# Sixteen short steps of dummy transposes in TensorE's list, and three other banks, in a decay-attention and mixture kernel

## The chip, the cores and the metric

The kernel runs on one core of one Trainium2 chip. The metric is device time in microseconds (us) of one execution, the median over several runs. Five engines work side by side, each through its own list of instructions in order: TensorE (PE in the profile, with its weight loads as PEld), VectorE (DVE), ScalarE (ACT), GpSimd (POOL) and SyncE (SP), which issues most of the DMAs. They wait for one another through semaphores.

## The reference, cut to what matters

```python
# r, k, v: (4, 8, 768, 48); w, u: (8, 48)
for t in range(S):
    kt, vt, rt = (k[:, :, t], v[:, :, t], r[:, :, t])
    cur = np.einsum('bhd,bhe->bhde', u[None] * kt, vt)
    y[:, :, t] = np.einsum('bhd,bhde->bhe', rt, state + cur)
    state = w[None, :, :, None] * state + np.einsum('bhd,bhe->bhde', kt, vt)
x = y.transpose(0, 2, 1, 3).reshape(B, S, H * D)     # (4, 768, 384)
logits = x @ w_gate                                   # 4 experts, the 2 largest are kept
for e in range(E):
    q, k, v = x @ wq[e], x @ wk[e], x @ wv[e]         # 384 -> 64
    a = softmax(scale * q @ k.T, causal)              # 768 x 768
    out += gate[e] * (a @ v @ wo[e])
```

Everything is float32. The first part is a linear attention with a decay by channel; its output is the input of a mixture of four small softmax attentions with causal mask.

## The kernel before, in words

The sequence of each of the four batches is cut into six chunks of 128 rows, so there are 24 chunks, n = 0 to 23. The first part works chunk by chunk; its steps have names that begin with `a_`. The second part works on groups of three chunks, G = 0 to 7, with steps that begin with `m_`.

For chunk n the first part does this. `load_chunk`, `load_vh` and `load_vs` bring k, r and v. `a_decay` (L470) multiplies k and r with powers of w, `a_ku` (L479, POOL) forms the products for the row's own term. `a_transpose` (L497) turns k and r on TensorE, 16 short transposes on line L513 (for chunk 0 on L506 and L524), and copies them to SBUF on ScalarE as kt (L519), rt (L532) and rx (L536). `a_quarters` (L541) forms the scores inside the chunk (32 matmuls on L552) and the state sums (up to 32 on L560). `a_mask` (L565) masks the scores on VectorE (sm, L569), `a_own` (L488) forms the own term on VectorE (L492, L494), `a_sum` (L599) adds the state on VectorE (z, L608) and multiplies it for the next chunk on POOL (L612). `a_out` (L573) forms the output with 64 small matmuls on L585 and L589, `a_add` (L591) adds the own term on VectorE (L596). `a_xt` (L614) turns the result, six transposes on L620 into the two banks of a `psb` home; ScalarE copies it to xt_hi (L623); and `a_xl` (L626) subtracts on VectorE, reading the same two banks again, which gives xt_lo (L631).

The second part starts with `m_values` (L678; nine matmuls on L686 for each chunk), `m_proj` (L651; nine on L661), `m_gate`, `m_scores` (L738), `m_weigh`, `m_turn` (L770), `m_av` (L791) and `m_out`. `hi_v`, `lo_v` (L451, L453), `hi_qk` and `lo_qk` (L438) split the weights into two parts, on ScalarE and VectorE, in the same early stretch.

The order is written out by hand. `ORDER` (L16) is a list of words, each the name of a step with its arguments; a step that yields has several words. The loop at L839 goes through the words, and every instruction of a step is appended to the list of its engine at that moment. Behind a slash stand hexadecimal digits: the homes that the step takes, in turn, by `take` (L245). TensorE's outputs live in eight PSUM banks of 512 columns. A `ps` home is one bank. A `psb` home i is the two banks i and i+1, because both are cut from one tile:

```python
SHARED = {"ps": 512, "psb": 512}
        if name in SHARED:
            return whole[:, i * SHARED[name]:i * SHARED[name] + WIDTH[name]]
```

So `a_xt,0/0` writes columns of banks 0 and 1, and `a_quarters,2/45` writes bank 4 for its first parity and bank 5 for its second, with the parities alternating from the first matmul on. A step that writes a bank which an earlier word reads waits until that reading is done.

`keep` (L357) is a step with no result that anyone reads: it takes a bank and turns the identity matrix into it, four transposes of 128x128. The kernel before has one such step at the very start, `keep,2`, on L360, ahead of the warm-up matmuls (L319).

Of the kernel before, what the change touches and what calls it, by code (L numbers as in the profile page):

```python
# [27 lines left out]
load_qk,0/5 a_quarters,3/26 m_values,0,0/1 a_xt,2/4 a_xt,2 a_xl,2 a_decay,4,1 a_transpose,4/0 m_values,0,1/7 hi_qk,0  # L28
lo_qk,0 load_chunk,5 a_decay,5,0 a_own,3/1 load_chunk,5 a_decay,5,1 load_vs,3 a_ku,5/0 a_ku,5 m_values,0,2/4 load_vs,3
a_transpose,4/0 m_proj,0,1,0/5 a_transpose,4/02 a_mask,3/03 m_proj,0,1,0/1 m_values,0,1 a_sum,3 a_sum,3/0 m_values,0,2  # L30
make_after m_gate,0/001 m_values,0,1/1 load_vh,5 m_proj,0,0,1/1 m_proj,0,0,1/2 load_vh,4 load_chunk,6 m_proj,0,1,0
m_proj,0,0,0/7 a_own,5/00 m_values,0,2 m_proj,0,0,0/0 a_decay,6,0 m_proj,0,0,0 load_chunk,6 m_values,0,0 a_out,3 a_add,3
a_transpose,5/4 load_chunk,7 load_chunk,7 load_vs,5 load_vs,5 m_proj,0,0,1 a_transpose,5/1 a_ku,4/0 a_transpose,5/11
m_scores,0,0,2/37 m_scores,0,0,2/41 m_scores,0,0,2/34 a_quarters,4/62 a_mask,4/03 m_scores,0,0,0/31 m_scores,0,0,0/15
a_xt,3/4 a_xt,3/1 m_scores,0,0,0/03 load_o,0/6 make_sums,0 m_scores,0,0,2 a_quarters,5/7 load_vs,4 m_gate,0
m_scores,0,0,1/31 a_ku,6/1 hi_o,0 a_xl,3/1 m_values,1,0/4 a_sum,4 a_sum,4/2 a_decay,6,1 a_mask,5/12 load_vs,4
m_scores,0,0,1/20 m_scores,0,0,0 m_scores,0,0,0 m_gate,0/501 a_ku,4 a_sum,5 load_vs,6 a_out,4 m_proj,0,1,1/3 load_vs,6
m_scores,0,0,2 load_chunk,8 m_scores,0,0,1/47 m_scores,0,0,1 m_weigh,0,0/3 a_out,5 a_own,4/1 load_vh,8 m_values,1,0/0
a_add,4 a_xt,4/1 m_proj,0,1,1 a_ku,6 m_proj,0,1,1 m_weigh,0,0 m_turn,0,0,0/5 m_values,1,0/2 m_scores,0,0,1 a_xt,4
m_scores,0,1,2/43 m_turn,0,0,0/0 a_add,5 m_scores,0,1,1/07 a_xl,4 m_weigh,0,1/2 a_xt,5/1 a_xt,5 m_weigh,0,1  # L40
a_transpose,6/5 a_decay,7,0 a_transpose,6/0 m_scores,0,1,1/01 a_xl,5 m_values,1,1/0 load_o,1/2 hi_o,1 lo_o,1
a_transpose,6/20 m_values,1,1 m_values,1,1 m_scores,0,1,2/50 m_proj,1,1,0/1 a_decay,7,1 m_scores,0,1,1/15 m_proj,1,0,0/4
m_scores,0,1,2/22 m_scores,0,1,2 load_vh,6 a_own,6/21 load_chunk,8 m_scores,0,1,2 a_decay,8,1 m_turn,0,1,0/5
m_scores,0,1,0/07 m_scores,0,1,0/33 m_scores,0,1,1 a_decay,8,0 a_ku,8/0 m_scores,0,1,0/44 m_proj,1,1,0 m_proj,1,0,0/0
a_ku,8 m_proj,1,1,0 m_proj,1,0,0 m_scores,0,1,0 a_quarters,6/3 m_values,1,2/0 m_scores,0,1,1 a_mask,6/30 a_sum,6/2
a_sum,6 m_proj,1,0,1/7 m_weigh,0,2/2 m_turn,0,1,0/2 load_vh,7 m_values,1,2 m_gate,1/100 m_values,1,2 m_scores,0,1,0
m_weigh,0,3/0 a_transpose,8/5 m_proj,1,0,1/1 m_proj,1,0,1 a_out,6 load_chunk,9 a_transpose,8/0 a_sum,6/1
a_transpose,8/01 m_weigh,0,2 m_turn,0,2,0/0 load_vs,7 lo_o,0 m_scores,1,0,0/47 m_turn,0,2,0/4 load_chunk,9 m_weigh,0,3
m_turn,0,3,0/5 m_turn,0,3,0/1 a_ku,7/1 a_add,6 m_scores,1,0,0/56 m_scores,1,0,0/24 m_scores,1,0,0 a_decay,9,0
m_scores,1,0,2/20 m_scores,1,0,2/02 a_transpose,7/4 m_scores,1,0,0 m_av,7,1,0,3 a_xt,6/6 a_xt,6/0 m_scores,1,0,2/30  # L50
a_xl,6/0 load_chunk,10 m_proj,1,1,1/2 m_gate,1 m_gate,1/110 a_ku,7 a_transpose,7/1 a_transpose,7/10 a_own,7/60
m_proj,1,1,1 m_proj,1,1,1 m_values,2,0/3 m_scores,1,0,2 m_scores,1,0,1/40 m_scores,1,0,1/07 m_scores,1,0,1/11
a_quarters,7/7 m_scores,1,0,2 a_sum,7 m_values,2,0/0 m_scores,1,0,1 m_av,0,0,0,3/2 m_scores,1,0,1 make_sums,1
a_mask,7/10 m_weigh,1,0/1 load_chunk,10 m_av,0,0,0,3/1 m_av,0,0,0,3/0 m_values,2,0/0 a_quarters,8/45 m_av,0,1,0,3/0
a_mask,8/23 a_sum,7/0 a_sum,8 m_av,0,1,0,3/0 load_vh,10 load_vh,9 m_av,0,1,0,3/1 load_vs,7 a_out,7 a_add,7 m_weigh,1,0
m_turn,1,0,1/2 load_vs,8 m_turn,1,0,1/3 load_vs,8 load_vs,9 m_weigh,1,1/1 a_decay,10,1 a_own,8/1 m_scores,1,1,2/06
a_xt,7/2 a_xt,7 m_scores,1,1,2/03 a_out,8 m_turn,1,0,0/0 a_xl,7 m_scores,1,1,0/23 m_turn,1,0,0/5 a_add,8 m_weigh,1,1
a_sum,8/2 m_turn,1,1,1/4 m_scores,1,1,2/15 a_xt,8/0 a_xt,8 m_turn,1,1,1/0 a_decay,10,0 load_vs,9 m_scores,1,1,0/36
a_xl,8 m_out,0,1/6 m_turn,1,0,2/4 m_out,0,1/0 load_vh,11 m_turn,1,1,0/0 m_turn,1,0,2/2 m_turn,1,1,0/1 load_chunk,12
a_transpose,10/6 m_scores,1,1,0/22 a_transpose,10/1 m_scores,1,1,1/24 a_transpose,10/22 load_chunk,11 a_decay,11,0  # L60
a_decay,9,1 m_scores,1,1,1/47 m_scores,1,1,1/54 m_scores,1,1,2 m_out,0,0/0 m_out,0,0/1 a_quarters,10/21 m_turn,1,1,2/6
a_mask,10/20 a_ku,9/1 a_transpose,9/3 m_turn,1,1,2/4 m_proj,2,0,0/5 a_ku,10/0 a_ku,10 a_own,10/1 load_chunk,11
load_chunk,14 m_proj,2,0,1/0 a_decay,11,1 a_decay,12,0 a_ku,11/0 load_chunk,14 a_ku,9 a_transpose,9/0 a_transpose,9/11
a_quarters,9/67 m_proj,2,1,1/4 m_scores,1,1,0 m_out,0,1 a_sum,9 a_decay,14,1 load_vh,12 a_sum,9/1 m_proj,2,1,0/3
m_scores,1,1,2 m_proj,2,0,0/2 m_proj,2,0,0 a_sum,10 a_mask,9/31 a_out,9 m_scores,1,1,1 m_weigh,1,2/3 m_weigh,1,2
m_scores,1,1,0 m_scores,1,1,1 m_proj,2,1,1/0 m_proj,2,0,1/0 m_proj,2,1,0 m_weigh,1,3/0 m_weigh,1,3 m_proj,2,1,0
# [810 lines left out]
```

## Time and profile before

| what | value |
|---|---|
| runs | 305.86 us median of 3 (305.4 to 306.49) |
| the profiled execution's own time | 306.47 us |
| its span (first to last instruction) | 304.7 us |
| busy PE / DVE / ACT / POOL | 292.3 / 206.0 / 213.6 / 173.2 us |
| mean granted TensorE clock | 0.976 of full speed |
| chain that ended last | PE 80%, DVE 6%, ACT 5%, issue 2%, POOL 1% |

The profile page has the busy time of each engine, the span in 40 slices of 7.6 us with the clock that was granted to TensorE in each, and the chain of work that ended last. The trace behind it can be asked for the instructions of an engine in order of time, for the busy time and clock of any stretch, and for who waited for whom. [...]

### The profile page before, as it was taken

The page shows a single profiled execution, that of the slowest core. Times are in us where ns is not written, and L with a number is a line of the kernel's source. Part 1 is how long each engine was busy: PE and PEld are TensorE (multiplying, and loading weights), DVE is VectorE, ACT ScalarE, POOL GpSimd, SP SyncE. Part 2 cuts the span into 40 slices and gives each one's busy share as a digit, 9 for nine tenths or more (in the row PEclk, how much of TensorE's full clock was granted, in tenths as well). Part 3 has the DMA queues.
Part 4 walks back from the last instruction along what each step waited for, and adds up shares of the span by engine and source line. Part 5 has one row for each costly group of instructions (what it writes and reads, how often), then busy time and mean ns, then how long its engine had stood idle before and what let it go on. Part 6 is the DMA issues. An engine that isn't in the chain of part 4 may idle for free.

```text
span 304.7 us, 13045 instructions
## 1 busy us (share of the span) xinstructions
PE 292.3 (96%) x5518; PEld 248.8 (82%) x5518; DVE 206.0 (68%) x676; ACT 213.6 (70%) x509; POOL 173.2 (57%) x227
## 2 busy tenths in 40 slices
...
PEclk9965999999999999999999999999999999999999
...
GB/s 157 219 188 118 80 55 107 120 122 25 108 56 166 72 41 159 105 17 105 93 106 1 80 69 141 111 123 102 41 3 41 54 2 31 0 25 56 23 60 77
DMA packets 103310, 24.83 MB, mean 81 GB/s; under 512 B 99794, under 2 KB 103252, under 8 KB 103252
## 3 DMA queue, kind: packets, MB, share of 16 engines
...
q8 instruction: 43, 0.70, 1.0%
...
## 4 chain that ended last, share of the span: by engine, by line
PE 80%; DVE 6%; ACT 5%; issue 2%; POOL 1%; ACTq 0%; DVEq 0%; POOLq 0%
PE banks L661 16%; PE banks L791 11%; PE banks L738 10%; PE banks L686 9%; PE banks L770 8%; PE banks L589 4%; PE banks L552 4%; PE banks L585 4%; PE banks L814 4%; PE banks L513 3%; PE banks L816 3%; PE banks L815 3%; PE banks L560 2%; PE banks L620 2%; ACT rx L536 1%
## 5 line engine op out<-in xcount | busy, mean ns | idle before, releaser
L761 POOL TENSOR_SCALAR pr<-pr,f,gate 128x128 f32<-128x128 f32 (+5 forms) x96 | 67.7, 719 | 72.2 <-DVE f L755 48.7
L743 DVE CUSTOM_DVE_ANT_0 pr<-banks,after 128x256 f32<-128x256 f32 (+5 forms) x96 | 56.5, 620 | 26.7 <-PE banks L738 18.8
L748 ACT ACTIVATE pr<-pr,nm 128x512 f32<-128x512 f32 (+5 forms) x96 | 63.4, 663 | 8.1 <-DVE nm L743 7.7
L773 ACT ACTIVATE pt<-banks 128x768 f32<-128x768 f32 (+1 forms) x64 | 45.6, 731 | 14.8 <-PE banks L770 14.1
L738 PE MATMUL banks<-tk,tq 64*128 64x384 f32 (+3 forms) x384 | 41.5, 338 | 0.2
L791 PE MATMUL banks<-pt,vv 128*64 128x384 f32 (+2 forms) x324 | 40.7, 393 | 0.7 <-DVE yl L800 0.7
L791 PEld LDWEIGHTS banks<-pt,vv 128*64 128x64 f32 x324 | 20.6, 136 | 16.6 <-issue 12.3
L661 PE MATMUL banks<-xt_hi,wqk_hi 128*128 128x384 f32 x96 | 33.5, 349 | 0.6 <-DVE nm L743 0.6
L738 PEld LDWEIGHTS banks<-tk,tq 64*128 64x128 f32 x384 | 30.7, 186 | 3.5 <-issue 1.4
L770 PE MATMUL banks<-ident,pr 64*128 64x64 f32 x672 | 31.6, 227 | 0.9 <-DVE xt_lo L631 0.5
L661 PE MATMUL banks<-xt_hi,wqk_lo 128*128 128x384 f32 x96 | 32.3, 337 | 0.0
L661 PE MATMUL banks<-xt_lo,wqk_hi 128*128 128x384 f32 x96 | 32.3, 336 | 0.0
L770 PEld LDWEIGHTS banks<-ident,pr 64*128 64x128 f32 x672 | 26.2, 139 | 7.1 <-issue 4.2
L612 POOL TENSOR_TENSOR z<-z,w 128x192 f32<-128x192 f32 x20 | 10.1, 506 | 30.4 <-DVE z L608 19.4
L483 POOL TENSOR_TENSOR ku<-kdbuf,uw 128x384 f32<-128x384 f32 x24 | 25.0, 1045 | 2.6 <-DVE banks L492 1.9
L476 POOL TENSOR_TENSOR rdbuf<-rdbuf,tab_r 128x384 f32<-128x384 f32 x22 | 22.7, 1038 | 5.7 <-DMA rdbuf<-in_r_dram 5.7
L585 PE MATMUL banks<-vhbuf,sm 64*64 64x48 f32 x384 | 25.7, 226 | 0.1
L485 POOL TENSOR_TENSOR ku<-ku,rdbuf 128x384 f32<-128x384 f32 x24 | 24.9, 1039 | 1.3
L585 PE MATMUL banks<-vsbuf,sm 64*64 64x48 f32 x384 | 25.2, 226 | 0.0
L686 PE MATMUL banks<-wv_hi,xt_hi 128*128 128x260 f32 x72 | 22.4, 312 | 0.1
L585 PEld LDWEIGHTS banks<-vhbuf,sm 64*64 64x64 f32 x384 | 21.5, 141 | 0.3 <-issue 0.3
L476 POOL TENSOR_TENSOR kdbuf<-kdbuf,tab_k 128x384 f32<-128x384 f32 x21 | 21.5, 1027 | 0.0
(125 smaller groups left out, 723.9 us busy)
## 6 DMA issues: line engine op xcount, KB each, us to landing
...
```

The costliest lines, as they stand in the source:

```text
L476: nc.gpsimd.tensor_tensor(t[:, :, :D], t[:, :, :D], (tab_k, tab_r)[which], op=OP.mult)
L483: nc.gpsimd.tensor_tensor(ku, kd[:, :, :D], uw, op=OP.mult)
L585: nc.tensor.matmul(o, st["sm", n][par][rows, p // 2, i], values, start=fresh, stop=True)
L661: nc.tensor.matmul(ps, a[:, t, m0:m0 + P], x[:, t, :], start=i == 0, stop=i == n - 1)
L686: nc.tensor.matmul(ps, x[:, t, cols], a[:, t, :], start=m == 0, stop=m == n - 1)
L738: nc.tensor.matmul(ps[par][:, n0:n1], tq[rows, part, q], tk[rows, key, n0:n1], start=i == 0, stop=i == 2)
L743: nc.vector.tensor_tensor_reduce(pr_[:, :N], ps[par], after[:, S - N:], 1.0, 3e38, op0=OP.add, op1=OP.min, accum_out=nm)
L748: nc.scalar.activation(pr_[:, :N], pr_[:, :N], AF.Exp, bias=nm, scale=-1.0, accum_out=sums[:, e, j, 0:1])
L761: nc.gpsimd.tensor_scalar(p[:, :N], p[:, :N], f[:, i], gate[:, i, e:e + 1], op0=OP.mult, op1=OP.mult)
L770: nc.tensor.transpose(both[:, x, half], mg[G]["p", e, j][rows, i * C:(i + 1) * C], ident[rows, rows])
L773: nc.scalar.activation(pt.rearrange("s (x half c) -> s x half c", x=n, half=2), both, AF.Copy)
L791: nc.tensor.matmul(psy[par * HD:par * HD + HD, j0 * C:j1 * C], vv[:, i % GC, e, :], mg[G]["t", e, i][:, (j0 - max(0, i - g * GC)) * C:(j1 ...
```

## The change

Sixteen steps `keep,50` to `keep,65` are put into `ORDER`, and `keep` makes two transposes for them in place of four, 32 transposes in all. Two steps stand between `a_quarters,1` and `a_xt,0`, five between `a_quarters,2` and `a_out,1`, six between `a_out,1` and `a_xt,1`, and three between `a_out,2` and `m_values,0,0`, seen from TensorE's list. No other word changes its place. Three words get other homes: `a_quarters,1` takes banks 7 and 0 in place of 2 and 7, `a_xt,0` takes `psb` home 5 (banks 5 and 6) in place of home 0 (banks 0 and 1), and `a_own,1` takes the second `ownv` buffer in place of the first. `a_quarters,2/45` keeps banks 4 and 5, and `a_xl,0` stands ahead of it in the list as before.

```diff
-load_vh,1 a_quarters,1/27 a_sum,0 a_sum,0/0 a_own,0/0 a_add,0 a_mask,1/12 a_ku,2/0 a_ku,2 a_transpose,2/0
-a_transpose,2/02 load_vh,2 a_xt,0/0 a_own,1/0 load_chunk,3 a_xt,0/0 load_vs,1 a_sum,1 a_sum,1/1 load_chunk,3 a_xl,0/0
-load_vs,1 a_quarters,2/45 a_mask,2/30 a_decay,3,1 a_sum,2 a_out,1 a_add,1 a_xt,1/0 load_v/6 hi_v load_vh,3 a_decay,3,0
-a_ku,3/1 a_ku,3 a_transpose,3/2 load_chunk,4 lo_v load_vs,2 load_vs,2 a_sum,2/2 a_out,2 a_own,2/1 a_add,2
-a_transpose,3/0 a_transpose,3/21 a_xt,1 m_values,0,0/3 load_qk,1/3 hi_qk,1 a_xl,1 lo_qk,1 load_chunk,4 a_decay,4,0
...
+load_vh,1 a_quarters,1/70 a_sum,0 a_sum,0/0 a_own,0/0 a_add,0 a_mask,1/12 a_ku,2/0 a_ku,2 a_transpose,2/0
+a_transpose,2/02 load_vh,2 keep,50/1 keep,51/2 a_xt,0/5 a_own,1/1 load_chunk,3 a_xt,0/0 load_vs,1 a_sum,1 a_sum,1/1
+load_chunk,3 a_xl,0/0 load_vs,1 a_quarters,2/45 a_mask,2/30 a_decay,3,1 a_sum,2 keep,52/1 keep,53/2 keep,54/3 keep,55/6
+keep,56/1 a_out,1 a_add,1 keep,57/2 keep,58/3 keep,59/6 keep,60/1 keep,61/7 keep,62/2 a_xt,1/0 load_v/6 hi_v load_vh,3
+a_decay,3,0 a_ku,3/1 a_ku,3 a_transpose,3/2 load_chunk,4 lo_v load_vs,2 load_vs,2 a_sum,2/2 a_out,2 a_own,2/1 a_add,2
+a_transpose,3/0 a_transpose,3/21 a_xt,1 keep,63/6 keep,64/7 keep,65/6 m_values,0,0/3 load_qk,1/3 hi_qk,1 a_xl,1 lo_qk,1
...
     def keep(i):
         ps = take("ps")
-        for _ in range(4):
+        for _ in range(2 if i >= 50 else 4):
             nc.tensor.transpose(ps[:, :P], ident, ident)
```

## Rows read from the trace of the kernel before

**Rows 1.** The page: busy time of the engines with its share and instructions, the granted clock in 40 slices, and the chain by engine.

```profile
PE 292.3 (96%) x5518; PEld 248.8 (82%) x5518; DVE 206.0 (68%) x676; ACT 213.6 (70%) x509; POOL 173.2 (57%) x227
...
PEclk9965999999999999999999999999999999999999
...
PE 80%; DVE 6%; ACT 5%; issue 2%; POOL 1%; ACTq 0%; DVEq 0%; POOLq 0%
```

**Rows 2.** Windows: busy time of the engines in stretches that end where TensorE pauses or its clock changes; first the stretch and its length, then each engine's busy us with its instructions, then the granted clock, the DMA share and GB/s.

```profile
14.46:16.18 1.72, 0.00 (x1) 0.01 (x1) 0.64 (x3) 0.99 (x3) 1.64 (x4) 1.00 0.74 140
16.18:17.00 0.82, 0.82 (x31) 0.70 (x35) 0.31 (x1) 0.05 (x1) 0.82 (x1) 1.00 0.79 182
17.00:22.36 5.36, 4.12 (x128) 3.54 (x125) 4.52 (x14) 2.83 (x7) 3.12 (x5) 0.50 0.96 201
22.36:25.57 3.21, 3.21 (x86) 3.04 (x86) 2.17 (x2) 1.65 (x4) 3.13 (x4) 0.50 0.88 167
25.82:30.50 4.68, 4.68 (x87) 4.36 (x89) 3.86 (x7) 1.30 (x3) 4.68 (x5) 0.50 0.46 90
30.75:50.00 19.25, 19.25 (x441) 17.73 (x439) 17.37 (x61) 14.67 (x41) 10.38 (x15) 1.00 0.29 60
...
50.00:100.00 50.00, 49.34 (x1047) 42.60 (x1043) 38.81 (x122) 38.04 (x88) 37.26 (x46) 1.00 0.52 107
100.00:200.00 100.00, 98.97 (x1948) 84.07 (x1947) 65.34 (x228) 71.38 (x174) 60.24 (x75) 1.00 0.41 86
200.00:300.00 100.00, 99.00 (x1536) 83.05 (x1535) 61.60 (x212) 73.36 (x173) 43.28 (x57) 1.00 0.15 40
```

**Rows 3.** TensorE in order of time: start, us from the first start to the last end of a merged row, line, tiles, shapes, count, and the idle time before it with what ended it.

```profile
16.18 0.40 PE L560 MATMUL banks<-vhbuf,kdbuf 64*48 64x48 f32 x16 [1.72 <-issue]
16.50 0.40 PE L620 MATMUL banks<-ident,ownv 64*128 64x64 f32 x6
16.83 1.03 PE L552 MATMUL banks<-rt,kt 48*64 48x64 f32 x32
...
18.88 0.74 PE L589 MATMUL banks<-z,rt 48*64 48x48 f32 x5 [0.39 <-DVE z L608]
...
21.31 0.31 PE L585 MATMUL banks<-vsbuf,sm 64*64 64x48 f32 x2
22.36 0.58 PE L620 MATMUL banks<-ident,ownv 64*128 64x64 f32 x6 [0.74 <-DVE ownv L596]
```

**Rows 4.** VectorE in order of time, columns as in rows 3.

```profile
16.69 0.76 DVE L569 TENSOR_TENSOR sm<-banks,before 128x256 f32<-128x256 f32 x2 [1.56 <-PE banks L560]
...
18.48 0.74 DVE L608 TENSOR_TENSOR z<-banks,z 128x192 f32<-128x192 f32 x2
19.14 0.55 DVE L631 TENSOR_TENSOR xt_lo<-banks,xt_hi 128x384 fp32r<-128x384 f32 x1
...
22.22 1.42 DVE L451 TENSOR_TENSOR wv_lo<-pr,wv_hi 128x768 fp32r<-128x768 f32 x1
23.56 0.96 DVE L453 TENSOR_TENSOR wv_lo<-wg,wv_hi 128x12 fp32r<-128x12 f32 x1
```

**Rows 5.** TensorE in order of time, the transposes of 128x128: those of `keep,2` with the first warm-up matmul behind them, and chunk 0's with the first of the tables' behind them; columns as in rows 3.

```profile
3.02 1.08 PE L360 MATMUL banks<-ident 128*128 128x128 f32 x4 [3.02 <-DVE banks L352]
3.90 0.63 PE L319 MATMUL banks<-pr 128*128 128x512 bf16 x1
...
7.05 0.60 PE L524 MATMUL banks<-ident,rdbuf 128*128 128x128 f32 x4
7.49 0.27 PE L393 MATMUL banks<-ident,vv 128*128 128x128 f32 x1
```

**Rows 6.** The chain of work that ended last, in order of time: start, us, what. The granted clock is 0.50 for what starts before 30.6 and 1.00 for what starts later.

```profile
22.95 0.87 PE banks L513 x16
...
25.82 2.32 PE banks L686 x9
28.13 1.06 PE banks L552 x32
29.20 0.64 PE banks L560 x32
29.84 0.51 PE banks L620 x6
30.35 0.67 PE banks L513 x16
31.02 2.35 PE banks L686 x18
...
39.15 0.65 PE banks L513 x16
...
40.37 0.62 PE banks L552 x32
40.99 0.36 PE banks L560 x32
...
50.66 0.20 PE banks L620 x6
```

**Rows 7.** TensorE in order of time: the first and the last row of `a_out,2` (64 matmuls at 0.50) and of `a_out,3` (64 at 1.00).

```profile
23.73 0.46 PE L589 MATMUL banks<-z,rt 48*64 48x48 f32 x8
...
25.38 0.31 PE L585 MATMUL banks<-vsbuf,sm 64*64 64x48 f32 x2
...
38.00 0.33 PE L589 MATMUL banks<-z,rt 48*64 48x48 f32 x8
...
38.92 0.23 PE L585 MATMUL banks<-vsbuf,sm 64*64 64x48 f32 x2
```

**Rows 8.** ScalarE in order of time, the copies of `a_xt,0` and of `a_transpose,3`.

```profile
16.95 0.49 ACT L623 ACTIVATE xt_hi<-banks 128x384 fp32r<-128x384 f32 x1 [1.48 <-PE banks L620]
...
23.89 0.60 ACT L519 ACTIVATE kt<-banks 128x512 f32<-128x512 f32 x1 [3.96 <-PE banks L513]
...
24.98 0.78 ACT L536 ACTIVATE rx<-banks 64x256 f32<-64x256 f32 x2
```

**Rows 9.** Windows of a quarter of a us, TensorE alone: stretch, length, busy us with instructions, granted clock, DMA share, GB/s.

```profile
17.00:17.25 0.25, 0.25 (x20) 0.52 1.18 268
...
30.50:30.75 0.25, 0.25 (x12) 0.68 0.00 0
30.75:31.00 0.25, 0.25 (x11) 1.00 0.04 9
```

More of the change, by code (lines that the diff above doesn't have):

```diff
@@ L27 @@
-a_transpose,3/0 a_transpose,3/21 a_xt,1 m_values,0,0/3 load_qk,1/3 hi_qk,1 a_xl,1 lo_qk,1 load_chunk,4 a_decay,4,0
[L28 to L66, printed above, removed]
@@ L132 @@
-m_scores,5,0,1/24 a_add,20 a_xt,20/0 m_scores,5,0,1/34 m_av,4,0,0,3/6 m_gate,5 m_scores,5,0,2 a_quarters,21/3
-m_scores,5,0,1/50 m_scores,5,0,1 m_scores,5,0,0 m_scores,5,0,1 m_out,3,0 m_av,4,0,0,3/0 m_av,4,1,0,3/2 m_gate,5/400
-m_values,6,1/4 a_mask,21/01 m_weigh,5,1/0 a_sum,21 m_av,4,1,0,3/1 m_av,4,1,0,3/0 m_av,4,0,0,3/1 a_xt,20 a_xl,20
-m_values,6,1 a_out,21 m_scores,5,1,0/52 m_values,6,1 m_weigh,5,1 m_turn,5,1,2/0 a_add,21 m_weigh,5,0/3 load_vs,22
-m_weigh,5,0 m_turn,5,1,1/6 m_turn,5,1,2/0 a_transpose,22/3 a_transpose,22/0 m_turn,5,1,0/0 a_transpose,22/02
```

246 lines of the change are left out of this document (145 added, 101 removed).

## The prediction

> **What bounds the kernel now.** I read the page first: TensorE is busy 96% of the span, the chain that ended last is 80% TensorE's, and the granted clock is near full in all slices but the third and fourth [rows 1]. So I asked next for windows around that stretch. [...] In finer windows the clock is 0.52 right from 17.0 and the rise at about 30.6 [rows 9]. What it did before each: before the fall, the pause of 1.72 us and then 0.8 us of work; before the rise, 4.68 of 4.68 us busy from 25.82 on, while 3.21 of 3.21 us busy from 22.36 to 25.57, followed by a quarter of a us idle, had not raised it [rows 2]. Inside the slow stretch TensorE waits twice for VectorE, 0.39 us for z and 0.74 us for ownv [rows 3].
>
> After 30.75 TensorE idles only 0.66, 1.03 and 1.00 us in the windows of 50, 100 and 100 us [rows 2], and its pauses there wait for engines that work on TensorE's own outputs. So I take a delay of `m_values,0,1` (chain, 31.02 [rows 6]) as a delay of the end, one for one; if some pauses absorb part of it, I allow half a us for that.
>
> **The change, part by part.** Durations are from the profiled execution, so the sum is made on its own 306.47 us, 0.61 above the median of the runs shown (305.86). The 1.77 us between its span of 304.7 and 306.47 are untouched.
>
> *The dummies' price.* The same instruction is in the trace at both speeds: four of `keep,2` take 3.02 to 3.90, 0.22 us each, and chunk 0's four on L524 take 7.05 to 7.49, 0.11 us each [rows 5]. That the first were at half speed I take from this spacing. At a granted clock of 0.50 the trace has only the short transposes of L513, 16 in 0.87 us, 0.054 us each for half the columns [rows 6], which would make 0.11. I take 0.22 at 0.50, the same instruction, and 0.11 at 1.00; the low end stays for the range.
>
> *`keep,50` and `51`*: four transposes at 16.45, still at full clock, 0.44 us. They stand behind the pause of 14.46 to 16.18, which nothing in the change touches, so the fall at 17.0 stays. `a_xt,0` ends at about 17.2.
>
> *The moved homes.* `a_quarters,1` in banks 7 and 0 and `a_own,1` in the second buffer cost nothing: these were last used for chunk 0's transposes or not at all, and `a_own,2`, which now shares its buffer with `a_xt,1`, comes on VectorE only after `lo_v`, long after those transposes. `a_xt,0` is different. It now lies in banks 5 and 6, and the second matmul of `a_quarters,2` writes bank 5. `a_xl,0`, ahead of it in the list, reads bank 5: that is xt_lo on L631, which VectorE runs from 19.14 to 19.69, at the end of an unbroken row of `a_mask,1`, `a_own,1` and `a_sum,1` that runs on from when `a_quarters,1` is done [rows 4]. Its other input, xt_hi, would come by 17.75 in place of 17.44 [rows 8] and doesn't hold it. So nothing brings L631 forward, and `a_quarters,2`, which began at 16.83 [rows 3], begins at 19.75. This is a new wait of 2.5 us; behind it in TensorE's list stand the five dummies and `a_out,1`, and VectorE's `a_mask,2` waits for it too.
>
> *From there on*, with what the row of before says in brackets. `a_quarters,2` at half clock: 1.06 + 0.64 = 1.70 [rows 6], to 21.45 (18.5). `keep,52` to `56`, ten transposes, 2.2 us, to 23.65; the pause of 0.39 us that they stand in has gone into the wait. `a_out,1` from 23.65 (18.88). When does the clock rise? At the start TensorE worked without a break from 3.02, and the spacing halves by 7.05; later 4.8 us went by between 25.82 and the rise. Unbroken work now begins at 19.75, so the same 4 to 4.8 us give 23.8 to 24.6; I take 24.2. `a_out` takes 1.96 us at 0.50 and 1.15 at 1.00, first start to last end [rows 7], so `a_out,1` ends at 24.95 (21.6).
>
> `keep,57` to `60`, eight transposes, 0.88 us, to 25.85. They cover `a_add,1` (0.74 us from the end of `a_out,1` to `a_xt,1` [rows 3]), so that pause is filled and 0.14 us over. `keep,61` writes bank 7, which `a_add,1` reads, free by then; it and `keep,62` take 0.44 us more. `a_xt,1` from 26.3 (22.36), 3.95 late. `a_xt,1` (0.58) and `a_transpose,3` (0.87) took 1.45 us to 23.81; at full clock 0.2 to 0.25 + 0.65 = 0.9 [rows 3, 6], to 27.2 (23.81), 3.4 late. `m_values,0,0` takes bank 3, which ScalarE's copies on L519 to L536 must leave: 2.0 us from 23.81 to 25.82 [rows 6, 8], at any clock, so it starts at 29.2, still 3.4 late. `a_out,2` (1.15) and `keep,63` to `65` (six, 0.66) fit into these 2 us and cost nothing; at half clock they would need 3.2 us and wouldn't. `lo_v`, 2.3 us on VectorE from `a_add,1` on [rows 4], ends at about 28.0, in time.
>
> `m_values,0,0` takes 1.2 us (half of 2.35) in place of 2.32: 2.3 late. `a_quarters,3` 0.62 + 0.36 = 0.98 in place of 1.70: 1.55 late. `a_xt,2` and `a_transpose,4` 0.95 in place of 1.18: `m_values,0,1` at 32.35, 1.3 late [all rows 6]. So the earlier clock pays back 2.6 of the 3.95 us that the wait and the dummies put in, and no more is left to win, since before is at full clock from here. VectorE, moved with `a_xt,2`, has xt_lo and the split weights some 1.3 us later as well, no more. Sum: 306.47 + 1.3 = 307.8 us, 1.9 above the median.
>
> [...] The trace: the work before the rise at 30.6 ended in 0.8 us of transposes (L620 and L513, from 29.84 [rows 6]), and the rise came; at the start 0.88 us of transposes stood ahead of the warm-up matmuls. In neither did they stand alone. [...]
>
> **The rivals.**
> 1. *The clock rises later, at some 27.5 us.* For it: 3.2 us of small products without a break, 22.36 to 25.57, were not followed by a rise. Against: there a pause came behind them, here none does. `a_out,1` then ends at 25.6, eight dummies at 27.35, the next four at 27.8, `a_transpose,3` at 28.7 (4.9 late), `m_values,0,0` at 30.7; the same savings behind it as above (1.1, 0.7, 0.25) leave 2.9 late: 309.4 us.
> 2. *Not slower: the wait for xt_lo doesn't come.* It decides whether L552 of chunk 2 starts near 17.2 or 19.75. If the writes to bank 5 found it free, `a_quarters,2` would end at 18.9, the ten dummies at 21.1, the clock would be up by 21 (4.8 us after 16.18), `a_out,1` would end at 22.2, twelve dummies at 23.5, `a_transpose,3` at 24.45 (0.65 late), and the savings behind it (1.1, 0.7, 0.25) leave 1.4 early: 305.1 us. A clock that stays up in spite of the wait is near it: `a_out,1` ends at 23.0, `a_transpose,3` at 25.2, 1.4 late, less 2.05: 0.6 early, 305.9. Against the first: both the homes and the order of words; against the second: the pause ahead of 17.0 is unchanged, and 2.5 us more are idle.
> 3. *The dummies do nothing for the clock*, and are cost alone. All is at half clock: `a_out,1` to 25.6, twelve dummies to 28.25, `a_transpose,3` to 29.7, `a_out,2` and six dummies to 32.9, `m_values,0,0` 7 late, and the rise 4.8 us behind that: about 313 us.
>
> **How the numbers follow.** Chances: the forecast 0.52, with its own range from 306.7 (the ten dummies before the rise at 0.11 each, 0.6 us less, and a rise a us sooner, half a us less) to 308.6 (a rise a us and a half later, 0.8 more); rival 1 0.25; rival 2 0.15; rival 3 0.08. What a measurement of this kernel can tell from no change is about 0.3%, 0.92 us, so 304.94 to 306.78 counts as the same. Faster needs the better half of rival 2 and a little luck: 0.08. The same has the rest of rival 2 and the low end of the forecast's range: 0.17. Slower has the rest: 0.75. The range leaves out rival 3 and the far end of rival 2: 305.5 to 310.2.
>
> **What would show it.** Right: TensorE idle from about 17.2 to 19.7 ahead of L552 of chunk 2, released by VectorE's xt_lo on L631; dummies of 0.2 us each behind it; the clock at 1.00 near 24; `m_values,0,1` a good us later than 31.02; from there on the windows as before. Wrong: L552 of chunk 2 at 17.2; no fall at 17.0; or a delay at 32 us that is gone by 100.

## The result, and the profile after

The change takes 309.37 us (median of 4 runs, 309.3 to 309.61) against 306.18 (median of 4, 305.4 to 306.85) for the kernel before: a ratio of 1.0106, with a 95% interval of 1.008 to 1.0133. It is slower by 3.2 us. The forecast was 307.8, in a range of 305.5 to 310.2: direction and range hold, and the centre is 1.6 us too low. The profiled execution took 309.43 us (span 307.7), 2.96 more than the one of before. `ORDER` is one line longer, so every line behind it has a number one higher than before. A ratio and its interval leave out disturbed runs and are not the quotient of the two medians that stand beside them.

The page of the changed kernel, the lines that answer to [rows 1]: busy time, granted clock in 40 slices, chain by engine.

```profile
PE 293.7 (95%) x5550; PEld 249.4 (81%) x5550; DVE 206.0 (67%) x676; ACT 213.8 (69%) x509; POOL 172.7 (56%) x227
...
PEclk9969999999999999999999999999999999999999
...
PE 82%; DVE 6%; ACT 5%; issue 3%; DMA 2%; POOL 1%; ACTq 0%; DVEq 0%; POOLq 0%; SPq 0%
```

One slice in place of two is at a reduced clock, TensorE is busy 1.4 us more, and DMA has come into the chain with 2%. The same in windows, columns as in [rows 2]:

```profile
17.23:19.68 2.45, 0.88 (x8) 0.58 (x9) 2.33 (x6) 1.87 (x4) 0.47 (x2) 0.50 1.15 245
19.68:24.05 4.37, 4.37 (x84) 3.95 (x88) 1.38 (x4) 1.01 (x4) 4.21 (x6) 0.50 0.86 176
...
24.05:50.00 25.95, 25.80 (x656) 23.57 (x653) 22.52 (x68) 16.82 (x44) 15.81 (x21) 1.00 0.35 72
50.00:100.00 50.00, 48.33 (x1063) 42.76 (x1057) 37.92 (x119) 39.41 (x92) 35.36 (x44) 1.00 0.52 105
100.00:200.00 100.00, 98.94 (x1978) 82.74 (x1971) 66.44 (x232) 69.57 (x169) 62.37 (x78) 1.00 0.41 85
200.00:300.00 100.00, 98.92 (x1520) 82.94 (x1519) 62.48 (x213) 74.59 (x177) 43.57 (x58) 1.00 0.16 43
```

The clock is halved from 17.23 to 24.05, half as long as before (17.0 to 30.7). In its first 2.45 us TensorE works only 0.88; then it works without a break until the rise. Between 50 and 100 us it is busy 48.33 us where it was 49.34 [rows 2]: one us has been lost there, far behind the edit. TensorE in order of time, columns as in [rows 3], around the new wait, at the dummies and where the second part starts ("issue" behind an arrow means that the profile shows nothing that the engine waited for):

```profile
16.24 0.40 PE L561 MATMUL banks<-vhbuf,kdbuf 64*48 64x48 f32 x16 [1.81 <-issue]
16.57 0.66 PE L361 MATMUL banks<-ident 128*128 128x128 f32 x4
17.15 0.56 PE L621 MATMUL banks<-ident,ownv 64*128 64x64 f32 x6
17.64 0.47 PE L553 MATMUL banks<-rt,kt 48*64 48x64 f32 x2
19.68 1.02 PE L553 MATMUL banks<-rt,kt 48*64 48x64 f32 x27 [1.57 <-DVE xt_lo L632]
...
21.38 2.39 PE L361 MATMUL banks<-ident 128*128 128x128 f32 x10
23.70 0.47 PE L590 MATMUL banks<-z,rt 48*64 48x48 f32 x8
...
24.92 1.53 PE L361 MATMUL banks<-ident 128*128 128x128 f32 x12
26.38 0.40 PE L621 MATMUL banks<-ident,ownv 64*128 64x64 f32 x6
...
28.29 0.87 PE L361 MATMUL banks<-ident 128*128 128x128 f32 x6
29.31 0.39 PE L687 MATMUL banks<-wv_hi,xt_hi 128*128 128x260 f32 x1
...
32.40 0.39 PE L687 MATMUL banks<-wv_hi,xt_hi 128*128 128x260 f32 x1
```

`a_quarters,2` stops behind its first two matmuls, until VectorE's L632 has read bank 5. The dummies behind it take 0.23 us each (from 21.38 to 23.70, ten), those after the rise 0.12 (from 24.92 to 26.38, twelve). `m_values,0,1` starts at 32.40; in the trace of before the first of the same matmuls starts at 30.95:

```profile
30.95 0.39 PE L686 MATMUL banks<-wv_hi,xt_hi 128*128 128x260 f32 x1
```

The next loss is at 54 to 57 us. ScalarE, VectorE and TensorE of the changed kernel there, three lines of their timelines, and the transfer that ScalarE waits for (the last line: size, and median us from issue to landing):

```profile
54.31 0.53 ACT L461 ACTIVATE wo_hi<-pr 128x384 fp32r<-128x384 f32 x1 [0.81 <-DMA pr<-in_moe_wo_dram]
...
54.87 1.36 DVE L464 TENSOR_TENSOR wo_lo<-pr,wo_hi 128x384 fp32r<-128x384 f32 x1 [1.44 <-ACT wo_hi L461]
...
56.82 0.44 PE L662 MATMUL banks<-xt_hi,wqk_hi 128*128 128x384 f32 x1 [1.17 <-DVE nm L744]
...
pr<-in_moe_wo_dram SPq DMA_DIRECT2D x1, 192.0 KB, 4.1
```

And the kernel before, the same four lines:

```profile
51.94 0.52 ACT L460 ACTIVATE wo_hi<-pr 128x384 fp32r<-128x384 f32 x1
...
52.49 1.31 DVE L463 TENSOR_TENSOR wo_lo<-pr,wo_hi 128x384 fp32r<-128x384 f32 x1 [0.52 <-ACT wo_hi L460]
...
54.39 0.44 PE L661 MATMUL banks<-xt_hi,wqk_hi 128*128 128x384 f32 x1 [0.18 <-DVE nm L743]
...
pr<-in_moe_wo_dram SPq DMA_DIRECT2D x1, 192.0 KB, 2.8
```

The weights `wo` of the second expert land 4.1 us after their issue in place of 2.8; ScalarE's split of them waits, VectorE's half of the split waits for ScalarE, and `m_scores`' maxima on L744 stand behind it in VectorE's list. TensorE, which waits for these, pauses 1.17 us in place of 0.18. That makes the 1.45 us late of 30 us into 2.43 late at 56.82. Two more steps of about a quarter of a us, near 224 and 255 us, bring it to the 2.9 by which the span is longer; TensorE has no pause over 0.05 us there, the same instructions take longer.

### The profile page after: what moved, and what is told of

The parts are those of the page before. It is cut to its first block, busy times and chain, and to the rows that moved or that the text cites. A ratio compares the mean times of both kernels' runs of the same rounds, so it can differ in the third digit from the quotient of the medians.

```text
span 307.7 us, 13109 instructions
## 1 busy us (share of the span) xinstructions
PE 293.7 (95%) x5550; PEld 249.4 (81%) x5550; DVE 206.0 (67%) x676; ACT 213.8 (69%) x509; POOL 172.7 (56%) x227
## 4 chain that ended last, share of the span: by engine, by line
PE 82%; DVE 6%; ACT 5%; issue 3%; DMA 2%; POOL 1%; ACTq 0%; DVEq 0%; POOLq 0%; SPq 0%
PE banks L662 15%; PE banks L792 12%; PE banks L739 9%; PE banks L687 9%; PE banks L771 7%; PE banks L553 5%; PE banks L590 4%; PE banks L586 3%; PE banks L815 3%; PE banks L514 3%; PE banks L561 3%; PE banks L817 2%; PE banks L816 2%; ACT pt L774 1%; PE banks L621 1%
## 5 line engine op out<-in xcount | busy, mean ns | idle before, releaser
L744 DVE CUSTOM_DVE_ANT_0 pr<-banks,after 128x256 f32<-128x256 f32 (+5 forms) x96 | 56.5, 620 | 27.0 <-PE banks L739 19.0
L662 PE MATMUL banks<-xt_hi,wqk_hi 128*128 128x384 f32 x96 | 33.5, 349 | 1.5 <-DVE nm L744 1.5
L739 PEld LDWEIGHTS banks<-tk,tq 64*128 64x128 f32 x384 | 30.7, 186 | 3.6 <-issue 1.7
L662 PE MATMUL banks<-xt_hi,wqk_lo 128*128 128x384 f32 x96 | 32.3, 337 | 0.0
L662 PE MATMUL banks<-xt_lo,wqk_hi 128*128 128x384 f32 x96 | 32.3, 337 | 0.0
L484 POOL TENSOR_TENSOR ku<-kdbuf,uw 128x384 f32<-128x384 f32 x24 | 24.2, 1012 | 2.8 <-DVE banks L493 2.1
L486 POOL TENSOR_TENSOR ku<-ku,rdbuf 128x384 f32<-128x384 f32 x24 | 24.2, 1009 | 1.3
L586 PE MATMUL banks<-vhbuf,sm 64*64 64x48 f32 x384 | 23.9, 219 | 0.0
L586 PE MATMUL banks<-vsbuf,sm 64*64 64x48 f32 x384 | 23.8, 219 | 0.0
L477 POOL TENSOR_TENSOR kdbuf<-kdbuf,tab_k 128x384 f32<-128x384 f32 x21 | 22.2, 1058 | 0.0
L570 DVE TENSOR_TENSOR sm<-banks,before 128x256 f32<-128x256 f32 x48 | 17.9, 416 | 5.2 <-PE banks L561 5.2
```

The costliest lines, as they stand in the source:

```text
L477: nc.gpsimd.tensor_tensor(t[:, :, :D], t[:, :, :D], (tab_k, tab_r)[which], op=OP.mult)
L484: nc.gpsimd.tensor_tensor(ku, kd[:, :, :D], uw, op=OP.mult)
L586: nc.tensor.matmul(o, st["sm", n][par][rows, p // 2, i], values, start=fresh, stop=True)
L662: nc.tensor.matmul(ps, a[:, t, m0:m0 + P], x[:, t, :], start=i == 0, stop=i == n - 1)
L739: nc.tensor.matmul(ps[par][:, n0:n1], tq[rows, part, q], tk[rows, key, n0:n1], start=i == 0, stop=i == 2)
L744: nc.vector.tensor_tensor_reduce(pr_[:, :N], ps[par], after[:, S - N:], 1.0, 3e38, op0=OP.add, op1=OP.min, accum_out=nm)
```

## The experiments

All twelve compute the whole reference. Ratios are to the kernel before on the same chip. It took 306.41 us there (median of 25) beside the first four, 305.27 (27) beside the next four, and 305.09 (20) beside the two kernels with ten dummies.

**The homes alone.** Before, with the change's three homes and no dummies.

```diff
-a_quarters,1/27 ... a_xt,0/0 a_own,1/0
+a_quarters,1/70 ... a_xt,0/5 a_own,1/1
```

> The kernel before with the three moved homes alone (a_quarters,1 in banks 7 and 0, a_xt,0 in banks 5 and 6, a_own,1 in the second buffer) and no dummies. Both theories expect TensorE idle from about 17.2 to 19.7 us for xt_lo. Theory A, the wait is the cost and the dummies bring the clock up early: without them the clock rises no sooner than about 30 us, so this kernel is 1.5 to 2.5 us slower than before, near or even above half of what the change costs. Theory B, the clock rises some 4 to 5 us after the wait ends, dummies or not: rise near 24, and the earlier clock pays the wait back, -1.0 to +0.3 us against before; the change's cost would then be the dummies' own time.

Measured: 305.61 us (304.35 to 307.69), ratio 1.0016 [0.9965, 1.0067]. The wait is there alone, and the clock still falls:

```profile
15.18 0.40 PE L560 MATMUL banks<-vhbuf,kdbuf 64*48 64x48 f32 x16 [0.55 <-issue]
...
18.61 1.02 PE L552 MATMUL banks<-rt,kt 48*64 48x64 f32 x27 [2.45 <-DVE xt_lo L631]
...
30.21 0.39 PE L686 MATMUL banks<-wv_hi,xt_hi 128*128 128x260 f32 x1
...
17.90:28.14 10.24, 8.64 (x220) 8.20 (x221) 5.77 (x15) 4.06 (x10) 9.81 (x11) 0.50 0.96 195
```

Neither theory came out whole: the interval of the time, from 1.1 us shorter than before to 2.1 longer, decides little between A's 1.5 to 2.5 longer and B's 1.0 shorter to 0.3 longer, and the rise, at 28.14, is neither A's near 30 nor B's near 24. `m_values,0,1` starts at 30.21, earlier than in before. The pause called issue is 0.55 us here and 1.72 in the profile of before, for the same instructions: single executions differ in it.

**The dummies alone.** Before with the sixteen steps at the same places, in banks 3 and 6, and no other home changed.

```diff
+keep,50/3 keep,51/6 (ahead of a_xt,0/0)
+keep,52/3 keep,53/6 keep,54/3 keep,55/6 keep,56/3 (ahead of a_out,1)
+keep,57/6 keep,58/3 keep,59/6 keep,60/3 keep,61/6 keep,62/3 (ahead of a_xt,1/0)
+keep,63/6 keep,64/6 keep,65/6 (ahead of m_values,0,0/3)
```

> The kernel before with the same 32 dummy transposes in the same places, but in banks 3 and 6, so that no step of the kernel changes its home. Both theories expect L552 of chunk 2 back at about 17.2 us with no wait. Theory A (the new wait of 2 to 2.5 us is what costs): the clock rises between 20.6 and 24 us, m_values,0,1 starts 0.5 to 1.7 us earlier than the 31.0 of before, and the end is -0.7 to +0.5 us against before, as the late landing of the second output weight at 54 us still takes about 1.0. Theory B (the dummies themselves cost): still 1.5 us or more slower than before, with m_values,0,1 after 32 us.

Measured: 305.19 us (304.18 to 307.2), ratio 0.9995 [0.9957, 1.0032]. In the profile there is neither the wait nor the pause called issue in `a_quarters,1`, and the clock stays at 1.00:

```profile
15.53 0.66 PE L360 MATMUL banks<-ident 128*128 128x128 f32 x4 [0.54 <-ACT rx L536]
...
17.43 1.31 PE L360 MATMUL banks<-ident 128*128 128x128 f32 x10
...
19.86 1.53 PE L360 MATMUL banks<-ident 128*128 128x128 f32 x12
...
24.23 0.87 PE L360 MATMUL banks<-ident 128*128 128x128 f32 x6
24.86 0.37 PE L686 MATMUL banks<-wv_hi,xt_hi 128*128 128x260 f32 x1
...
14.00:30.00 16.00, 14.11 (x409) 12.48 (x402) 13.95 (x27) 9.79 (x22) 15.12 (x16) 1.00 0.77 157
```

The time is Theory A's; its rise between 20.6 and 24 us is not, as there was no fall. The mean granted clock was 0.998 or more in 8 of its 10 runs. By the 302.67 us that seven runs of before with a clock of 1.000 took in the mean, the median should then lie some 3 us below before (an estimate), and it doesn't: at full clock the dummies are longer than what they stand in. Ten of them (from 17.43 on, some 1.2 us) stand in a pause of 0.39 us, twelve (1.46) in one of 0.74 [rows 3], and `m_values,0,0` starts without a wait right behind the last six.

**The early `wo`.** The change, with `load_o,1` issued ahead of `load_vh,8`.

```diff
-a_own,4/1 load_vh,8 ... m_values,1,1/0 load_o,1/2 hi_o,1 lo_o,1
+a_own,4/1 load_o,1/2 load_vh,8 ... m_values,1,1/0 hi_o,1 lo_o,1
```

> The changed kernel with one DMA issue moved: load_o,1 stands ahead of load_vh,8, so that it is issued some 7 us sooner. Theory A (the 1.0 us that is lost between 52 and 57 us is the wait for this transfer, by ScalarE's wo_hi, VectorE's wo_lo and then TensorE): the pause of 1.2 us ahead of L662 at 56.8 shrinks to 0.2 or less and the kernel is 0.8 to 1.2 us faster than the change. Theory B (VectorE is late there for another reason): the pause stays and the time is the change's within 0.3 us.

Measured: 307.63 us (307.06 to 309.4), ratio 1.007 [1.0032, 1.0107]. The pause of 1.17 us is 0.20 again, and ScalarE no longer waits for the transfer. The first row is the start of `m_values,0,1`:

```profile
30.98 0.39 PE L687 MATMUL banks<-wv_hi,xt_hi 128*128 128x260 f32 x1
...
51.99 0.52 ACT L461 ACTIVATE wo_hi<-pr 128x384 fp32r<-128x384 f32 x1
...
54.46 0.44 PE L662 MATMUL banks<-xt_hi,wqk_hi 128*128 128x384 f32 x1 [0.20 <-DVE nm L744]
```

From `m_values,0,1` to this L662 it is 23.48 us here, 24.42 in the change and 23.44 in before. At one and the same mean clock (0.987 to 0.989) five of its runs have a mean of 308.2, eight of the change, in other batches, 309.26: the late `wo` is worth about 1 us, as the trace said.

**All 32 dummies at 44 us**, where the clock is long up.

```diff
-a_xl,3/1 m_values,1,0/4
+a_xl,3/1 keep,50/4 keep,51/4 ... keep,65/4 m_values,1,0/4
```

> The kernel before with the same 32 dummies, all ahead of m_values,1,0 at 43.7 us, at full clock, behind everything that the change touches. Their own time there is 32 x 0.11 = 3.5 us. Theory A (the second output weight lands late because 64 more instructions in TensorE's list move the fetch of its code, a 16 KB packet, to just ahead of that weight's packets): a delay of 3.5 us at 50 grows to about 4.5 at 57 us. Theory B (the late landing comes from the changed start of the kernel): 3.5 us at 50 and 3.5 at 57.

Measured: one run, 308.42 us. 32 transposes take 3.71 us in one block, and put in some 3.4 us. `wo` came in time (TensorE's pause behind it is 0.20 us), against Theory A: 64 more instructions in TensorE's list don't by themselves make `wo` late, as far as one execution tells. Two windows, the block with the first matmuls behind it, and what follows:

```profile
41.64:45.35 3.71, 3.71 (x36) 3.71 (x35) 3.17 (x16) 3.00 (x12) 3.25 (x4) 1.00 0.06 11
45.35:55.00 9.65, 9.65 (x215) 9.02 (x214) 5.83 (x15) 5.03 (x12) 4.59 (x9) 1.00 0.48 104
```

The clock holds through 3.7 us of almost nothing but transposes, and after them; it fell in before behind 1.72 us of pause.

**The change again**, on another chip.

```diff
(the changed kernel, nothing edited)
```

> The changed kernel once more, beside the others on one chip, to see how its time hangs on how long the clock is at half speed. From the mean granted clock of each execution of the kernel before, that kernel takes about 302.7 us without a half-speed stretch and about 306.4 with one of 13.65 us. Theory A (the change adds about 5 us of work and waits at equal clock, and the earlier rise gives about 2 of them back): 307 to 310 us, and the executions with the shortest half-speed stretch still at 306.5 or more. Theory B (its time is as the clock alone makes it): executions with a short half-speed stretch reach 303 to 304 us.

Measured: 309.11 us (308.67 to 310.65, 6 runs), ratio 1.0106 [1.007, 1.0142], the same ratio, and Theory A's range. Its pause called issue was 0.47 us, yet L553 again waited for xt_lo (1.87 us), the clock again fell (17.35 to 24.18), and L662 again paused 1.21 us for the late `wo`.

**Three edits that were to take away or fill the pause called issue.** The first issues `load_chunk,4` ahead of `load_v`; the second puts eight long bf16 matmuls into the list ahead of the pause; the third is the first with `load_o,1` moved as above.

```diff
-a_xt,1/0 load_v/6 hi_v ... a_transpose,3/2 load_chunk,4 lo_v
+a_xt,1/0 load_chunk,4 load_v/6 hi_v ... a_transpose,3/2 lo_v
```

> The kernel before, no dummies, homes as before; one DMA issue is moved: the k of chunk 4 stands ahead of the value weights, so that SyncE waits for its buffer (until about 11.5 us) before it queues more data. Theory A (the pause of 1.72 us at 14.46 is TensorE without code, whose 16 KB packet waits behind queued data, and this pause is what lets the clock fall): the packet starts by 12.5 us, the pause is under 0.5 us, the clock stays at 1.00 or falls in few executions, and the time is 302 to 304 us. Theory B (the pause has another cause, or the later waits of 0.4 and 0.7 us make the clock fall anyway): half-speed stretches as before, 305 to 307 us.

Measured: 304.72 us (303.1 to 306.71, 10 runs), ratio 0.9977 [0.9936, 1.0018]; a pause of 1.16 us is left, and the clock is halved from 19.87 to 30.11.

```diff
+def hold(i, n):
+    ps, warm = take("ps"), tables["warm"]
+    for _ in range(n):
+        nc.tensor.matmul(ps, warm[:, :P], warm[:, :512], start=True, stop=True)
...
-load_vh,1 a_quarters,1/27
+load_vh,1 hold,1,8/0 a_quarters,1/27
```

> The kernel before, homes as before, with eight long dummies in place of the 32 short ones and ahead of the pause: matmuls of 512 columns in bf16 on zeros in bank 0, between a_transpose,2 and a_quarters,1, 8 x 0.21 = 1.7 us at full clock. Theory A (TensorE has to wait for its code until about 16.2 us in any case, so that the work ahead of it costs nothing and only the idle time goes): a_quarters,1 ends near 16.5 as before, the clock doesn't fall at 17, 302.5 to 304.5 us. Theory B (the pause is shorter in other executions, or the dummies count in full): 304.5 to 306.5 us.

Measured: 306.46 us (304.97 to 306.77), ratio 1.0016 [0.999, 1.0043]. The pause is down to 0.33 us, and the clock falls nevertheless, at 19.37, for 10.24 us: the theory that this pause alone causes the fall falls with it. What stands just ahead of the fall here is the old wait for z, longer than in before (lines of this kernel are five higher):

```profile
19.22 0.74 PE L594 MATMUL banks<-z,rt 48*64 48x48 f32 x5 [0.99 <-DVE z L613]
```

```diff
-a_xt,1/0 load_v/6 hi_v ... load_chunk,4 lo_v ... load_vh,8 ... load_o,1/2 hi_o,1
+a_xt,1/0 load_chunk,4 load_v/6 hi_v ... lo_v ... load_o,1/2 load_vh,8 ... hi_o,1
```

> The kernel of kd4_first with the second output weight's DMA issued ahead of load_vh,8 as well. If the wait for that weight costs nothing without the moved code packet, as in before, the same as kd4_first within 0.4 us; if it costs in some executions, 0.3 to 1.0 us faster than kd4_first.

Measured: 304.54 us (303.12 to 306.97), ratio 0.9984 [0.9942, 1.0026]. No pause called issue in its profile, and a fall at 17.99 for 10.24 us all the same, again behind waits for VectorE, 0.49 us for ownv and this one:

```profile
17.53 0.72 PE L589 MATMUL banks<-z,rt 48*64 48x48 f32 x5 [0.64 <-DVE z L608]
```

So every execution without dummies in this stretch has idle time of TensorE ahead of the fall, be it the pause or waits. None of the three is distinguishable from before.

**Ten dummies in the two pauses**, with before's homes.

```diff
-a_sum,2 a_out,1 a_add,1 a_xt,1/0
+a_sum,2 keep,52/3 keep,53/6 a_out,1 a_add,1 keep,57/6 keep,58/3 keep,59/6 a_xt,1/0
```

> Before with ten of the dummies alone: two steps (four transposes) between a_quarters,2 and a_out,1, three steps (six) between a_out,1 and a_xt,1; all other homes as before. In dummies_only the clock was at 1.00 throughout and yet the time was that of before, because the dummies were longer than the pauses they stood in (ten in 0.39 us, twelve in 0.74, six in a pause that is none): some 2 us put in. Theory A (the clock is kept by TensorE working on through these pauses, and the surplus is what ate it): ten transposes at 0.11 us are 0.44 and 0.66 us, which the two pauses hide, so at most 0.3 us is put in; the clock stays at 1.00 in the profile, and the median is 303 to 304.5, ratio 0.990 to 0.995. Theory B (the clock's fall is set by the pause of some 1.7 us ahead of 16.2 us, which these dummies don't touch, and falls at another moment in each execution): the profile shows a half-speed stretch of 6 to 14 us somewhere between 17 and 31, dummies of 0.22 us, and the median is 305 to 306.5, ratio 0.997 to 1.002.

Measured: 305.04 us (302.78 to 306.19, 12 runs), ratio 0.9982 [0.9949, 1.0016]. The profile is Theory A's, at 1.00 throughout. Of the waits up to `a_xt,1` 0.18 us for z is left, with a pause called issue of 0.39 us in the middle of `a_out,1`:

```profile
17.14 0.66 PE L360 MATMUL banks<-ident 128*128 128x128 f32 x4
17.97 0.66 PE L589 MATMUL banks<-z,rt 48*64 48x48 f32 x5 [0.18 <-DVE z L608]
...
19.54 0.25 PE L589 MATMUL banks<-z,rt 48*64 48x48 f32 x1 [0.39 <-issue]
...
20.13 0.87 PE L360 MATMUL banks<-ident 128*128 128x128 f32 x6
20.93 0.40 PE L620 MATMUL banks<-ident,ownv 64*128 64x64 f32 x6
...
14.00:30.00 16.00, 14.06 (x417) 12.13 (x414) 14.91 (x30) 11.36 (x25) 15.27 (x16) 1.00 0.94 191
```

That execution took 302.78 us. The median missed Theory A's 303 to 304.5: the clock was 0.999 or 1.000 in 4 of the 12 runs only.

**The same with both transfers earlier.**

```diff
-a_xt,1/0 load_v/6 hi_v ... load_chunk,4 lo_v ... load_vh,8 ... load_o,1/2 hi_o,1
+a_xt,1/0 load_chunk,4 load_v/6 hi_v ... lo_v ... load_o,1/2 load_vh,8 ... hi_o,1
```

> few, with load_chunk,4's transfer issued ahead of load_v and load_o,1 ahead of load_vh,8. If the order of the transfers is worth what kd4_first and kd4_first_wo hinted at (0.2% each over before, inside their intervals) and adds to few: 0.3 to 1 us below few, the fastest median of all. If it was the clock's scatter alone: within 0.3 us of few at an equal mean granted clock.

Measured: 303.12 us (302.24 to 305.2, 9 runs), ratio 0.994 [0.9903, 0.9976]: below both kernels, and the only one here whose interval lies wholly below before. Its profile (302.92) is no shorter than the last one's: what it has is that none of its nine runs had a mean clock under 0.992. That the earlier transfers keep the clock up is not shown by this; nine runs beside twelve may differ by chance.

**Two more executions of the ten dummies**, to see what those with a lower clock have.

```diff
(the kernel with ten dummies, nothing edited)
```

> few once more, unchanged, for a second profiled execution of it. In few's runs the clock was at 1.00 in four of twelve and below in the others. Theory A (what differs between executions is TensorE's pause that the profile calls issue, in the middle of a_quarters,1, which was 0 to 1.8 us long in the profiles so far): an execution at 1.00 shows no such pause; one at 0.983 to 0.994 shows a pause of 0.3 us or more there, and the fall of the clock within some us behind it. Theory B (the fall doesn't depend on it): a fall without the pause, or the pause without a fall.

> The same as few_look1, for a third profiled execution: Theory A a pause called issue of 0.3 us or more in a_quarters,1 if and only if the clock falls; Theory B one without the other.

Measured: 304.09 and 304.22 us, clock 0.994 in both; a run of before beside them took 306.76. Theory A holds in both. The first, its pause and its halved stretch in windows:

```profile
15.90 0.40 PE L560 MATMUL banks<-vhbuf,kdbuf 64*48 64x48 f32 x16 [1.42 <-issue]
...
14.48:15.90 1.42, 0.00 (x0) 0.00 (x0) 0.64 (x3) 0.99 (x3) 1.42 (x3) 1.00 0.61 117
16.78:20.19 3.41, 3.41 (x106) 2.99 (x98) 3.29 (x10) 2.78 (x7) 1.44 (x3) 0.50 1.19 255
```

and the second:

```profile
16.64 0.40 PE L560 MATMUL banks<-vhbuf,kdbuf 64*48 64x48 f32 x16 [2.06 <-issue]
...
17.50:20.91 3.41, 3.41 (x104) 2.99 (x99) 3.29 (x10) 2.79 (x7) 1.15 (x2) 0.50 1.05 226
```

With the pause (1.42 and 2.06 us) the clock falls here too, at 16.78 and 17.50 us where it was 17.0 in before, but TensorE works on through all of the halved stretch and it ends after 3.41 us in place of 13.65.

**The fourteen profiled executions side by side**: the pause called issue in `a_quarters,1`, where the clock fell, and how long it stayed at 0.50.

| kernel | dummies | wait for xt_lo | pause, us | fall at, us | half clock, us |
|---|---|---|---|---|---|
| before | none | no | 1.72 | 17.0 | 13.65 |
| load_chunk,4 early | none | no | 1.16 | 19.87 | 10.24 |
| eight long matmuls | ahead of the pause | no | 0.33 | 19.37 | 10.24 |
| load_chunk,4 and wo early | none | no | none | 17.99 | 10.24 |
| all dummies at 44 us | later | no | 0.37 | 21.16 | 6.83 |
| homes alone | none | 2.45 | 0.55 | 17.90 | 10.24 |
| the change | 32 | 1.57 | 1.81 | 17.23 | 6.83 |
| the change again | 32 | 1.87 | 0.47 | 17.35 | 6.83 |
| the change, wo early | 32 | 2.10 | none | 18.68 | 3.41 |
| ten dummies, second execution | 10 | no | 1.42 | 16.78 | 3.41 |
| ten dummies, third execution | 10 | no | 2.06 | 17.50 | 3.41 |
| dummies alone | 32 | no | none | no fall | 0 |
| ten dummies | 10 | no | none | no fall | 0 |
| ten dummies, both early | 10 | no | none | no fall | 0 |

Without dummies in this stretch the clock falls whether the pause is there or not. With dummies it falls only in the executions that have the pause or the wait for xt_lo. Each row is one execution. What makes the pause long, short or absent stays open.

**The time by the mean granted clock**, mean us of the runs of a kernel with a clock in the column, and how many (before in the three batches named above, without two runs of 530 and 666 us):

| kernel | 0.976 to 0.978 | 0.981 to 0.983 | 0.987 to 0.989 | 0.992 to 0.994 | 0.998 to 1.000 |
|---|---|---|---|---|---|
| before | 306.72 (25) | 305.60 (24) | 304.58 (14) | | 302.67 (7) |
| homes alone | 307.67 (2) | 305.73 (3) | 306.3 (1) | 304.67 (4) | |
| dummies alone | | | | 307.04 (2) | 304.99 (8) |
| the change, both batches | | 310.65 (1) | 309.26 (8) | 308.9 (1) | |
| the change, wo early | | 309.4 (1) | 308.22 (5) | 307.12 (4) | |
| load_chunk,4 early | 306.50 (2) | 305.33 (3) | 304.46 (3) | | 303.15 (2) |
| eight long matmuls | | 306.64 (5) | 305.78 (5) | | |
| load_chunk,4 and wo early | 306.27 (1) | 305.27 (6) | 304.13 (2) | | 303.12 (1) |
| all dummies at 44 us | | | 308.42 (1) | | |
| ten dummies | | 306.19 (1) | 305.04 (1) | 305.03 (6) | 303.45 (4) |
| ten dummies, both early | | | | 303.92 (3) | 302.89 (6) |

Before alone spreads over 4 us in these means, with the clock; but a column is not one time either, at 0.983 its runs go from 304.6 to 307.0. At an equal clock of 0.987 to 0.989 the change is 4.7 us above before; that its clock is more often that high gives back about 2 of it (306.72 to 304.58). Of the 4.7, the dummies alone account for some 2.3 (304.99 against 302.67, at full clock), the late `wo` for about 1, and the homes alone for 0.1 to 1.7 (three columns, one to three runs in each); that these add up is an estimate, as no run has them together at one clock. Ten dummies cost little at full clock (three of the four runs took 302.8 to 302.9, the fourth 305.2), and held it in 4 runs of 12, where before has it in 7 of 70. One thing is not settled: the ten dummies' runs at 0.994 lie in two heaps, 304.1 to 304.3 (two of the six, and the two later executions) and 305.0 to 305.9 (four), and no profile caught the upper one.

## Why the prediction was right, and where it was off

**The wait.** Right in place, releaser and end: `a_quarters,2` goes on at 19.68, forecast 19.75, released by xt_lo on L632. `a_xt,0` ended at 17.7, not 17.2, and two matmuls of `a_quarters,2` ran ahead (the first writes bank 4; why the second, which by the code writes bank 5, ran too stays open), so the idle time is 1.57 us, less than the 2.5 named; the end of the wait, on which the sum went, is the same.

**The dummies' price.** Right: 0.23 us at 0.50 against the 0.22 taken, 0.12 at 1.00 against 0.11. The low bound of 0.11 at half clock is refuted.

**The rise.** Forecast 24.2, measured 24.05, 0.35 us into `a_out,1`, which ends at 24.92 against 24.95. That the fall would come at 17.0 in spite of `keep,50` and `51` is right for this execution: it came at 17.23, with the pause of 1.81 us ahead of it. The ground for it, "which nothing in the change touches", was too strong: the pause is 1.72 us in one execution and absent in others of nearly the same code, as the table shows.

**The way to `m_values,0,1`.** `a_xt,1` at 26.38 (forecast 26.3), `m_values,0,0` at 29.31 (29.2), `m_values,0,1` at 32.40 (32.35). The term "the earlier clock pays back 2.6 of the 3.95 us" came out (4.02 late at `a_xt,1`, 1.45 at `m_values,0,1`); as before has that at 30.95 or, in the chain, 31.02, the delay is 1.4 us.

**The step that was off** is "I take a delay of `m_values,0,1` (chain, 31.02 [rows 6]) as a delay of the end, one for one", with half a us allowed for pauses that absorb part of it. The allowance had the wrong sign: nothing was absorbed, and 1.5 us were added. Its ground was that TensorE's later pauses wait for engines that work on TensorE's own outputs; the one at 56.82 comes, by way of VectorE and ScalarE, from a transfer. One us is this late `wo` at 54 us, which the early `wo` shows by taking it away (1.17 to 0.20 us of pause, about 1 us of time at an equal clock). The other half, the steps near 224 and 255 us, was not tried, and its cause is open. Why `wo` lands late is argued, not shown: in the trace's packet records a fetch of code starts just ahead of `wo`'s packets in the change (51.1 and 51.6 us), while in before these are through by 51.2. (The page of before has them in the line `q8 instruction: 43, 0.70, 1.0%`, 43 packets with 0.70 MB, some 16 KB each. That they are TensorE's is the author's estimate, from their number beside its 5518 matmuls: one to 128.) In three of the eleven profiled executions that have `load_o,1` in its old place such a fetch is under way when `wo`'s first packet starts, in the change, the change again and the dummies alone, and there `wo` lands 4.1, 4.6 and 3.7 us after its issue (in the last without a longer pause of TensorE, 0.21 us); in the other eight none is, and it lands in 2.8 to 3.3. That is an agreement: no run moved the fetch, and the dummies at 44 us, which were to do so, did not bring it ahead.

**The sum against the median.** The profile of before, with a halved stretch of 13.65 us, is of its slower kind (25 of the 70 runs have a clock as low), and the seven with a mean clock of 1.000 took 302.67 in the mean. So the base of the sum had in it some 4 us that come and go. The forecast of +1.3 was one against that base, and the credit of 2.6 us for the earlier rise is whole only against such executions. How near a median of before lies to this base is chance: 306.18 in the result, 305.09 to 306.41 in the later batches.

**The rivals.** The first had a figure of 309.4 us, next to the result, by a rise at 27.5 that did not come: the agreement is chance. The second, no wait, is refuted in place for the change (the row at 19.68), but the dummies alone show what it would have been: 305.2, forecast 305.1. That agreement is chance too: the rival had a fall and a rise by 21, and `m_values,0,1` 1.4 us early; the profile has no fall, and it starts at 27.94, 3.0 early. The third is refuted: the clock rose 0.3 us behind ten transposes, and held through 32 of them at 44 us. In the three profiled executions with the wait and the dummies it rose at 24.05, 24.18 and 22.09, in the one with the wait and no dummies at 28.14.

**Transposes and the clock.** The rows of the dummies at 44 us: 3.71 us busy with 36 matmuls, 32 of them transposes, at 1.00, and 9.65 us at 1.00 behind them. So a clock that was up stayed up through the float32 transposes of this kernel. That transposes alone would raise a clock that is down, no run here shows.
